# Another hand-written order for a fused retention and SoLU kernel: the same steps, rearranged over five engines

## The chip, the cores and the metric

The kernel runs on one core of a Trainium2 chip. A core has five engines that run their own instruction streams in order: PE (matrix multiplies and transposes), DVE (vector), ACT (scalar functions), POOL (GpSimd) and SP, which here only issues DMA transfers. They meet through semaphores. The metric is the device time of one execution in microseconds; the median of three runs before the change was 212.04 us (211.69 to 212.27).

## What is computed

Two parts follow each other. A retention layer works on q, k and v of 8 batches, 8 heads, 576 positions and 64 columns; its output, 4608 tokens of 512, goes through a feed-forward block with a SoLU activation and a layer norm.

```python
scores = scale * np.matmul(q, k.transpose(0, 1, 3, 2))
gamma = 1.0 - 2.0 ** (-5.0 - np.arange(H, dtype=np.float32))
Dmat = np.where(rel >= 0, gamma[:, None, None] ** rel[None, :, :], 0.0)
ret = scores * Dmat[None, :, :, :]
x = np.matmul(ret, v)
...
h = x @ w_in
sm = exp(h - max(h)) / (sum(exp(h - max(h))) + 1e-09)
solu = h * sm
ln = (solu - mean(solu)) / np.sqrt(var(solu) + 1e-06) * g_ln
out = ln @ w_out
```

The last six lines are shortened; `h` has 1024 columns, `out` has 512.

## The kernel before

The 4608 tokens are cut into 36 chunks of 128. For each pair of batches there are nine: four chunks of each batch in turn, and a ninth that holds the last 64 tokens of both. Each chunk passes through the same chain of steps, and each step is a small function with a two-letter name:

- `lq`, `lk`, `lv`: SP loads q, k and v of the chunk (256 KB each). `li` and `lo` load the four slices of w_in and of w_out (512 KB each).
- `cq`, `cv`: scale by a table of gamma powers and round to 16 bits; `ck`: round only. The engine is written behind the name: `a` ACT, `v` DVE, `g` POOL.
- `tq` (PE) transposes q and k into a PSUM bank, `eq` copies both halves out; `tr` and `er` do so for q alone where k is transposed by a DMA (`kd`, and `kq` for q).
- `sc` (PE, line 391) makes the scores in two PSUM banks, `mk` (DVE, line 404) masks them in two halves, `av` (PE, line 466) multiplies with v.
- `kv` (PE), `ad` (DVE), `dk` and `d3` (POOL) carry the running state of keys and values to the next chunk; `fs` (PE) adds its share to the output of `av`; `ex` copies the result out as xT.
- `m1` (PE, line 258) makes h, 128 by 1024, in one of two PSUM buffers; `mr` does the same in four parts, for the first two chunks, as the slices of w_in come in, each cast by `wi`.
- `mx` (DVE, line 522) takes the maximum, `xp` (ACT, line 528) the exponential, `so` (DVE, line 537) the product u, `sq` (ACT) the squares. The first five chunks are centred by `ce` (DVE); for the others, centred weights take its place.
- `tu` and `eu` transpose u through PE and copy it out; `du` does so by a DMA.
- `m2` (PE, line 258) multiplies with w_out, `st` (ACT) scales by the normalization and SP stores the chunk. The normalization is made by `ra` (a pair of small instructions, lines 576 and 582) and `rp` (POOL, line 591).
- `wo` scales w_out by g_ln, `mm` and `mc` make its mean over the rows, and the eight `ws` (line 831) subtract that mean: the centred weights w_c, which `m2` takes from chunk 5 on.
- The last chunk is worked in halves: `hm`, `hx`, `hp`, `ho`, `hc`, `ht`, `he`, `hq`, `h2`, `hw`.

The order is written out by hand in the string `ORDER`: 1021 tokens of the form step:chunk:engine, run from left to right under a manual schedule. Each engine gets its instructions in that order and executes them in that order; a step that waits holds up all that stand behind it on its engine. SP issues loads, stores and transposing DMAs in the same way, so a store that waits for its data holds up the loads behind it. Two more strings are consumed alongside: `BANKS` names one of four PSUM banks for each allocation in turn, and `SLOTS` names the buffer in a ring for each tile. A new tile in a bank or slot waits until the last reader of the old one is done.

Of the kernel before, what the change touches and what calls it, by code (L numbers as in the profile page):

```python
# [28 lines left out]
so:1 ce:1 mx:0 fs:2 tq:3 dk:2 ex:2:a d3:2 eq:3:a lk:8 sq:1 m1:2 cv:3:g ad:4 xp:0 mx:2 kv:3 av:4
fs:4 lq:7 ck:5:g ad:3 sc:3 cq:5:g so:0 ex:4:a mk:3 tq:5 tu:1 dk:3 xp:2 dk:4 lq:10 cv:5:g d3:3  # L30
eq:5:a lv:7 cq:6:g lq:11 m1:4 sc:5 d3:4 wu:3:1 wo:1:g cv:6:g wo:5:g wo:0:g av:3 wo:3:g eu:1:a
ce:0 wo:7:g so:2 mk:5 tu:0 mx:4 ck:6:a sq:0 eu:0:a fs:3 tq:6 ra:1:g av:5 fs:5 ra:0:g lq:8 ex:3:a
kv:5 lq:20 ad:5 eq:6:av rp:1 d3:5 m1:3 xp:4 cq:7:g kv:6 dk:5 rp:0 sc:6 ex:5:a ce:2 wo:4:a tu:2
lk:9 so:4 ad:6 m1:5 lq:9 mk:6 ce:4 sq:2 av:6 ra:2:g wo:2:a fs:6 wo:6:a mx:3 xp:3 lv:9 tu:4 lv:8
# [6 lines left out]
st:3 so:6 mk:9 fs:8 ck:12:a cv:12:g m2:5 ex:8:a av:9 sc:10 so:7 m1:8 sq:6 ex:9:v tu:7 cv:10:v  # L41
lv:20 mk:10 tu:6 cq:12:g st:5 m1:9 mx:8 ra:6:v sq:7 lv:14 lv:27 eu:6:a xp:8 eu:7:v lq:15 lk:14
kv:10 ad:10 av:10 kv:11 lv:13 lv:15 ck:13:g ex:10:a so:8 ra:7:g ad:11 mx:9 tq:11 rp:7 lv:21 m2:7
lq:16 lk:17 lk:18 lk:15 cq:17:g tu:8 eq:11:v sq:8 rp:6 eu:8:v m2:6 st:7 tq:12 sc:11 xp:9 eq:12:a
lk:20 ra:8:g so:9 m1:10 st:6 dk:9 sq:9 mk:11 cv:18:g d3:11 lq:23 av:11 mx:10 sc:12 fs:11 dk:11
ck:16:a xp:10 dk:10 mk:12 ex:11:a m2:8 rp:8 cq:13:g tu:9 av:12 st:8 lv:17 so:10 cq:14:g ra:9:g
# [46 lines left out]
0123102310102310321032013203112032120312031312310213002130213023013021032102313210213012301320132032  # L93
3012032031231023120311203132012310321032130210320130021302123012032103210320120123012302130213012301
30121320101320313012303123102310320
# [7 lines left out]
vf 012345601234560125436154164305216425  # L103
kf 012345012345012340152341503215401235
qf 012345601234560135260315246031564023
k16 012345021345023145021543210541403251
q16 012340123401204312431201204413410421
v16 012340132401324301340132410140312432
t 01231021302132013201320132012310
qkT 012302130213102310231203213213102310  # L110
s16 012312031203102310230123012031203
ret0 012302130213021302130213021302130123
ret1 012302130213021302130213021302130123
# [762 lines left out]
```

## Time and profile before

| | us |
|---|---|
| median of three runs | 212.04 |
| the profiled execution | 212.92 |
| its span, first to last instruction | 210.6 |
| PE busy | 191.4 |
| DVE busy | 180.7 |
| ACT busy | 167.1 |
| POOL busy | 167.8 |
| bytes moved by DMA | 47.97 MB |

A row of the page's groups gives line, engine, operation, the tile written and those read, shapes and count; behind the bar stand busy time, mean duration in nanoseconds, and idle time of the engine just before, with what ended it. In the chain of waits and in the timeline each row begins with start and length in microseconds; a bracket at the end of a timeline row gives the idle time before it and what ended it. One matmul step as `m1` is recorded as 16 instructions that overlap, so durations of PE are read from start to start.

### The profile page before, as it was taken

The page shows a single profiled execution, that of the slowest core. Times are in us where ns is not written, and L with a number is a line of the kernel's source. Part 1 is how long each engine was busy: PE and PEld are TensorE (multiplying, and loading weights), DVE is VectorE, ACT ScalarE, POOL GpSimd, SP SyncE. Part 2 cuts the span into 40 slices and gives each one's busy share as a digit, 9 for nine tenths or more (in the row PEclk, how much of TensorE's full clock was granted, in tenths as well). Part 3 has the DMA queues.
Part 4 walks back from the last instruction along what each step waited for, and adds up shares of the span by engine and source line. Part 5 has one row for each costly group of instructions (what it writes and reads, how often), then busy time and mean ns, then how long its engine had stood idle before and what let it go on. Part 6 is the DMA issues. An engine that isn't in the chain of part 4 may idle for free.

```text
span 210.6 us, 7529 instructions
## 1 busy us (share of the span) xinstructions
PE 191.4 (91%) x3091; PEld 122.7 (58%) x3091; DVE 180.7 (86%) x303; ACT 167.1 (79%) x293; POOL 167.8 (80%) x252
## 2 busy tenths in 40 slices
PE   0387889899889999999999999999999999999992
PEld 0353566665656667566666566675664665655571
DVE  0366999999999997998999899999999899899730
ACT  2266799789867788799888789999896999878961
POOL 3455999999999499899989999699939999851530
PEclk9999999999999999999999999999999999999998
DMA  6999999999999999999848999999899999993942
GB/s 156 306 300 248 257 284 347 244 241 228 210 291 336 232 238 234 282 241 253 243 110 242 191 207 267 224 266 162 179 237 178 207 219 240 162 265 85 239 157 100
DMA packets 111858, 47.97 MB, mean 228 GB/s; under 512 B 95560, under 2 KB 105808, under 8 KB 111824
## 3 DMA queue, kind: packets, MB, share of 16 engines
q1 hardware_dynamic: 111504, 47.33, 96.7%
q8 instruction: 24, 0.39, 0.8%
q10 hardware_dynamic: 320, 0.16, 0.3%
q14 instruction: 10, 0.08, 0.1%
HBM read 32.54 MB, written 9.44 MB: 199 GB/s over the span
## 4 chain that ended last, share of the span: by engine, by line
PE 69%; DVE 15%; SPq 6%; DMA 4%; ACT 2%; issue 1%; POOL 1%; ACTq 0%; DVEq 0%
PE o L258 26%; PE h L258 23%; PE tp L253 5%; PE sc L391 4%; DMA vf<-in_v_dram 4%; DVE nm L522 4%; DVE u L537 3%; PE x L466 3%; PE x L258 3%; SPq L270 3%; DVE ret L404 3%; PE lp L253 3%; DVE w_c L831 2%; PE kp L415 2%; SPq L274 1%; SPq L789 1%
## 5 line engine op out<-in xcount | busy, mean ns | idle before, releaser
L258 PE MATMUL h<-w_in,xT 128*64 128x512 f16 x560 | 68.6, 385 | 1.9 <-ACT w_in L245 0.9
L258 PE MATMUL o<-w_c,uT 128*64 128x512 f16 x480 | 56.7, 380 | 0.0
L404 DVE TENSOR_TENSOR ret<-sc,tris 128x512 f16<-128x512 f32 x72 | 46.0, 681 | 1.8 <-PE sc L391 1.3
L258 PEld LDWEIGHTS <-xT 128*64 128x64 f16 x576 | 31.4, 111 | 25.4 <-issue 3.0
L528 ACT ACTIVATE e<-h,nm 128x1024 f32<-128x1024 f32 x35 | 39.1, 1117 | 8.7 <-DVE nm L522 7.4
L258 PEld LDWEIGHTS <-uT 128*64 128x64 f16 x560 | 31.3, 110 | 22.6 <-issue 0.4
L537 DVE SCALAR_TENSOR_TENSOR u<-h,e 128x1024 f16<-128x1024 f32 x35 | 42.5, 1215 | 1.8 <-ACT e L528 1.7
L522 DVE TENSOR_REDUCE nm<-h 128x1 f32<-128x1024 f32 x35 | 42.6, 1216 | 1.0 <-PE h L258 0.9
L288 POOL TENSOR_TENSOR v<-vf,small 128x512 f16<-128x512 f32 x32 | 33.7, 1059 | 10.1 <-DMA vf<-in_v_dram 7.7
L565 ACT ACTIVATE sq<-u,su 128x1024 bf16<-128x1024 f16 x30 | 34.5, 1149 | 3.0 <-DVE u L537 2.9
L442 POOL TENSOR_TENSOR s<-t,small 128x512 f16<-128x512 f32 x32 | 33.1, 1043 | 1.7 <-DVE t L430 1.5
L299 POOL TENSOR_TENSOR q<-qf,small 128x512 f16<-128x512 f32 x30 | 32.0, 1071 | 0.3
L245 ACT COPY qkT<-tp 128x512 f16<-128x512 f16 x45 | 24.3, 591 | 9.4 <-PE tp L253 9.3
L625 ACT ACTIVATE o_sb<-o,rs 128x512 f32<-128x512 f32 x35 | 24.0, 687 | 5.6 <-POOL rs L591 2.4
L591 POOL TENSOR_TENSOR rs<-w,mhalf 128x1 f32<-128x1 f32 x36 | 20.2, 563 | 4.7 <-DVE su L685 3.2
L253 PE MATMUL tp<-ident,q 128*64 128x128 f16 x248 | 13.1, 229 | 9.5 <-DVE q L299 7.7
L253 PEld LDWEIGHTS <-q 128*64 128x64 f16 x280 | 11.2, 115 | 13.1 <-DVE q L299 8.2
L245 ACT CAST xT<-x 128x512 f16<-128x512 f32 x25 | 14.7, 587 | 4.1 <-PE x L258 2.5
L391 PE MATMUL sc<-qkT 64*128 64x128 f16 x288 | 14.6, 225 | 1.6 <-ACT qkT L245 1.0
L466 PE MATMUL x<-ret,v 128*64 128x128 f16 x288 | 14.6, 222 | 0.9 <-DVE ret L404 0.8
L582 POOL TENSOR_SCALAR w<-ss,w 128x1 f32<-128x1 f32 x24 | 6.4, 265 | 11.1 <-ACT sq L565 8.8
L454 POOL TENSOR_TENSOR s<-t,small 128x256 f32<-128x256 f32 x24 | 14.8, 620 | 0.2
(86 smaller groups left out, 273.3 us busy)
## 6 DMA issues: line engine op xcount, KB each, us to landing
vf<-in_v_dram SPq DMA_DIRECT2D x36, 256.0 KB, 5.2
kf<-in_k_dram SPq DMA_DIRECT2D x36, 256.0 KB, 5.1
qf<-in_q_dram SPq DMA_DIRECT2D x36, 256.0 KB, 5.1
out_dram<-o_sb SPq DMA_DIRECT2D x35, 256.0 KB, 3.9
w_in<-in_moe_w_in_dram SPq DMA_DIRECT2D x4, 512.0 KB, 5.9
w_out<-in_moe_w_out_dram SPq DMA_DIRECT2D x4, 512.0 KB, 6.5
uT<-u SPq DMA_TRANSPOSE x18, 3.9
out_dram<-o_sbh SPq DMA_DIRECT2D x2, 64.0 KB, 2.1
```

What stands on the lines that cost most here:

```text
L245: (engine.copy if engine is nc.scalar else engine.tensor_copy)(out=out, in_=in_)
L253: nc.tensor.transpose(out=out[w], in_=in_[:, w], identity=ident)
L258: nc.tensor.matmul(out=out[w], lhsT=lhsT[:, w], rhs=rhs, start=start, stop=stop, skip_group_check=True,)
L288: engine.tensor_tensor(out=dst, in0=T.pop((key, n)), in1=table.unsqueeze(2).to_broadcast([P, H, D]), op=ALU.mult,)
L299: ENG[e].tensor_tensor(out=dst.rearrange("p (a h) d -> p h a d", h=2), in0=T.pop(("qf", n)).rearrange("p (h a) d -> p h a d", h=2), in1=ta ...
L404: nc.vector.tensor_tensor(out=r, in0=s, in1=m, op=ALU.mult)
L442: nc.gpsimd.tensor_tensor(out=s16, in0=t.unsqueeze(2).to_broadcast([P, 4, 2, D]), in1=gd.unsqueeze(3).to_broadcast([P, 4, 2, D]), op=ALU.mult,
L522: nc.vector.tensor_reduce(out=nm, in_=T["h", n], axis=AX.X, op=ALU.max, negate=True)
L528: nc.scalar.activation(out=e, in_=T["h", n], func=ACT.Exp, bias=T.pop(("nm", n)), accum_out=s)
L537: nc.vector.scalar_tensor_tensor(out=u, in0=T.pop(("h", n)), scalar=-1.0, in1=T.pop(("e", n)), op0=ALU.mult, op1=ALU.mult, accum_out=su,)
L565: nc.scalar.activation(out=s, in_=T.pop(("v", n)), func=ACT.Square, scale=-float(DFF), bias=T.pop(("su", n)), accum_out=ss,)
L625: nc.scalar.activation(out=o_sb, in_=T.pop(("o", n)), func=ACT.Copy, scale=T.pop(("rs", n)))
```

## The change

Only `ORDER`, `BANKS` and `SLOTS` are new; no function is touched. Both orders have 1021 tokens and the same steps on the same chunks. What differs is where a step stands, and for 63 of them on which engine it runs. Counted by engine (`eq` has two halves, each with its engine):

| step | before: ACT, DVE, POOL | after: ACT, DVE, POOL |
|---|---|---|
| ck | 18, 1, 17 | 17, 4, 15 |
| cq | -, 5, 31 | -, 3, 33 |
| cv | -, 4, 32 | -, 2, 34 |
| eq (halves) | 45, 17, - | 45, 17, - |
| er | 3, 1, - | 4, 0, - |
| ex | 25, 11, - | 29, 7, - |
| eu | 10, 7, - | 9, 8, - |
| ra | -, 7, 29 | -, 14, 22 |

`wi` and `ws` keep their counts; ws:2 and ws:0 swap POOL and DVE. The ra moved to DVE are those of chunks 5, 7, 18, 20, 25, 29, 32 and 35; that of chunk 26 goes to POOL.

The order of the first loads, and the steps up to the place where the prediction looks:

```diff
-c1:0 lv:1 lk:1 lq:2 lq:1 ck:1:g cq:1:v lk:2 lq:0 cv:1:v li:3 lk:0 cq:2:g lv:0 lq:4 li:0 ck:2:g
-li:2 lk:4 cv:0:g tq:1 kv:1 ad:1 eq:1:a ck:0:a sc:1 wi:3:1:v dk:1 li:1 cq:0:v tq:2 mk:1 eq:2:a
...
-kv:0 eq:0:a mr:1:3 ad:0 dk:0 wi:0:0:a wi:2:1:a mk:2 sc:0 mk:0 c2:0 d3:0 mr:1:0 wi:1:1:v ck:4:a
-d3:1 mr:1:2 wi:1:0:a tq:4 av:0 mr:1:1 ex:0:v lk:6 lv:5 cv:4:g mr:0:0 cv:2:g mx:1 eq:4:a lq:6 lo:0
...
-ex:6:a cq:10:g eu:2:v cv:7:g ck:7:v so:3 mx:5 sq:4 ra:4:g rp:2 lk:10 dk:6 lv:12 rp:4 m2:1 mm:0
-tq:7 mc:0:v eq:7:a xp:5 ce:3 m1:6 ck:9:g eu:4:v ws:4:g sc:7 ck:8:a cq:9:g st:1 ws:2:g lk:13 sq:3
-m2:0 lv:10 ws:3:v mk:7 lk:11 lk:12 lv:11 st:0 so:5 ck:10:g lq:12 ws:1:v lv:18 cv:8:g av:7 ra:3:g
-kv:7 fs:7 ad:7 cq:8:v ex:7:a sq:5 m2:2 dk:7 tq:8 cv:9:v lq:17 st:2 mx:6 eq:8:a rp:3 tu:5 tu:3
-cq:11:g lq:14 lk:16 kv:9 ws:5:v ad:9 ws:7:v ck:11:g m1:7 ws:6:v sc:8 eu:5:a eu:3:a m2:4 mx:7 xp:6
-lq:13 mk:8 cv:11:g ws:0:v xp:7 tq:9 d3:9 st:4 tq:10 m2:3 eq:10:a ra:5:g rp:5 eq:9:v av:8 sc:9
...
-hm:35:1 ra:31:v rp:30 st:30 m2:31 so:34 rp:31 hx:35:0 hx:35:1 sq:34 hp:35:0 rp:32 hp:35:1 ho:35:0
-rp:33 du:34 ho:35:1 m2:33 st:31 ht:35:0 m2:32 st:33 ra:34:v hc:35 hq:35:0:v he:35:0:v ht:35:1
-rp:34 hq:35:1:a he:35:1:v m2:34 st:32 ra:35:g h2:35:1 rp:35 h2:35:0 st:34 hw:35:1:v hw:35:0:a
+c1:0 lk:1 lv:1 ck:1:v lq:0 lq:1 lk:2 lq:2 cv:1:g ck:2:a li:3 lv:0 lk:0 kv:1 li:0 li:2 cq:1:v lq:4
+lk:4 ad:1 wi:3:0:a tq:1 eq:1:v sc:1 gt:0 li:1 mk:1 cq:0:g wi:3:1:v lv:4 lv:2 d3:1 cq:2:g tq:2
...
+wi:0:1:g eq:0:av lk:6 kv:0 ad:0 wi:0:0:a wi:2:0:v wi:2:1:a wu:3:1 lq:6 sc:0 mr:1:0 lo:0 ck:4:a
+mk:0 mr:1:2 wi:1:0:a cq:4:g dk:0 lv:6 av:0 wi:1:1:v d3:0 tq:4 mr:1:1 ex:0:v lo:1 mr:0:3 lo:2
...
+m1:5 av:6 ce:4 rp:1 ad:6 wo:2:a wo:4:a wo:6:a mx:3 dk:6 cv:7:g eu:2:a lq:8 tu:4 xp:3 eu:4:v fs:6
+ra:2:g rp:0 m2:1 rp:2 ex:6:a ck:7:a mx:5 lv:9 mm:0 tq:7 lv:11 lq:9 xp:5 so:3 lk:9 lk:10 cq:9:g
+mc:0:v eq:7:a ck:9:g st:1 ck:8:a ck:10:g ce:3 ws:6:v lv:8 lk:16 m1:6 sc:7 lq:18 sq:4 lk:11 sq:3
+ws:0:g ws:1:v ra:3:g ws:2:v ws:4:g lq:17 lq:12 mk:7 m2:0 cq:8:v st:0 rp:3 kv:7 ad:7 ra:4:g lk:13
+lk:17 av:7 lv:10 lk:12 cv:8:g so:5 fs:7 rp:4 lv:12 m2:2 ex:7:a tu:3 ws:5:v lq:14 st:2 ws:3:v tq:8
+dk:7 eq:8:a lv:18 cq:11:g cv:9:v tu:5 eu:3:v kv:9 cv:11:g m1:7 cq:12:g ad:9 ws:7:v mx:6 sq:5 sc:8
+mx:7 eu:5:a m2:4 xp:6 mk:8 ra:5:v tq:10 eq:10:v lq:13 xp:7 lq:15 so:6 tq:9 eq:9:a m2:3 sc:9 st:4
...
+rp:31 m2:31 rp:30 ra:32:v ra:33:g st:30 so:34 du:34 hx:35:0 sq:34 st:31 hx:35:1 m2:33 hp:35:0
+hp:35:1 m2:32 ho:35:0 ho:35:1 rp:32 hc:35 ra:34:v rp:33 rp:34 st:33 ht:35:1 ht:35:0 he:35:1:v
+he:35:0:v m2:34 hq:35:0:v h2:35:1 st:32 hq:35:1:a h2:35:0 st:34 ra:35:v rp:35 hw:35:1:v hw:35:0:a
```

`BANKS` and `SLOTS` follow the new order, with other numbers throughout.

More of the change, by code (lines that the diff above doesn't have):

```diff
@@ L29 @@
[L29 to L34, printed above, removed]
@@ L41 @@
[L41 to L46, printed above, removed]
@@ new lines @@
+eq:4:a sc:4 cv:4:g cv:2:g mr:0:0 mx:1 xp:1 mr:0:2 lo:3 kv:2 mr:0:1 mk:4 lk:7 ad:2 so:1 ck:3:a
+cq:3:g av:2 fs:2 ex:2:a ce:1 mx:0 d3:2 lq:7 dk:2 tq:3 kv:4 cv:3:g ad:4 m1:2 kv:3 eq:3:a mx:2
+cq:5:g sq:1 ck:5:g d3:4 ad:3 av:4 dk:4 lq:10 xp:0 fs:4 sc:3 so:0 ex:4:a xp:2 cv:5:g tu:1 dk:3
+tq:5 d3:3 cq:6:g mk:3 wo:1:g eu:1:a m1:4 wo:0:g eq:5:a cv:6:g wo:3:g wo:5:g ck:6:a lq:11 wo:7:g
+ce:0 sq:0 ra:0:g sc:5 so:2 av:3 mk:5 ra:1:g fs:3 cq:7:g tu:0 ex:3:a eu:0:a tq:6 av:5 mx:4 cq:10:g
+kv:5 ce:2 eq:6:av lk:8 fs:5 m1:3 xp:4 ad:5 ex:5:a sc:6 dk:5 kv:6 d3:5 sq:2 lv:7 so:4 tu:2 mk:6
@@ new lines @@
+fs:11 st:6 sc:12 m2:8 sq:9 ra:9:g rp:9 ex:11:a xp:10 tu:9 cq:14:g mk:12 tq:13 so:10 st:8 lq:19
+av:12 fs:12 eq:13:a m1:11 eu:9:v ck:14:v kv:12 sc:13 lq:23 dk:11 d3:10 ad:12 mx:11 ex:12:a tq:14
+sq:10 d3:11 cq:17:g m2:9 eq:14:av tu:10 lv:17 mk:13 kv:13 cq:16:g m1:12 ad:13 lq:21 ra:10:g av:13
+xp:11 st:9 cv:14:g rp:10 cq:15:g eu:10:a ck:15:a fs:13 ck:17:a sc:14 so:11 sq:11 d3:12 m2:10
+ex:13:a dk:12 mx:12 mk:14 tq:15 cv:20:v xp:12 lv:16 tu:11 ra:11:g rp:11 lq:27 lk:21 so:12 eq:15:v
+kv:14 eu:11:a st:10 ad:14 m1:13 av:14 lv:23 mx:13 lk:26 fs:14 sc:15 cv:15:g m2:11 lv:19 mk:15
@@ new lines @@
+d3:13 dk:13 lk:22 d3:14 ck:18:a kv:15 sq:12 ad:15 cq:19:v ex:14:a tu:12 tq:16 dk:14 tq:18 st:11
+ck:19:a dk:15 av:15 cq:20:g cq:21:g xp:13 eq:16:v lk:27 fs:15 cv:16:g ex:15:a m1:14 eu:12:v tq:17
+sc:16 so:13 eq:18:a lq:24 m1:15 eq:17:a mx:14 mk:16 cv:18:g kv:16 ra:12:g ad:16 lq:22 tu:13 sc:17
+dk:16 xp:14 mx:15 eu:13:a mk:17 sq:13 ra:13:v m2:12 av:16 ck:21:v tq:19 fs:16 ck:20:g cv:17:g
+rp:12 so:14 lk:24 xp:15 cq:27:g lk:23 cv:21:g m2:13 ex:16:a kv:18 st:12 eq:19:av tq:21 rp:13
+m1:16 ad:18 cv:19:g av:17 sq:14 fs:17 eq:21:va tq:20 so:15 mx:16 tu:14 st:13 kv:19 ra:14:g
@@ new lines @@
+ex:17:a ad:19 dk:19 eq:20:av dk:18 rp:14 xp:16 sq:15 lv:25 eu:14:v tu:15 ra:15:g so:16 lq:29
+d3:18 du:16 lv:28 cq:23:g lq:26 eu:15:a lq:25 lv:30 m1:17 ck:24:a sc:18 lv:24 sq:16 cq:22:g mk:18
+lv:22 lq:28 m2:14 rp:15 ck:27:a av:18 lk:30 lk:28 mx:17 xp:17 m2:15 ex:18:v ra:16:g st:14 sc:19
+mk:19 rp:16 m1:18 ck:22:g st:15 av:19 so:17 ex:19:a sc:20 mk:20 m2:16 sq:17 mx:18 av:20 fs:20
+tu:17 kv:20 ck:23:a m1:19 eu:17:v ra:17:g ad:20 xp:18 st:16 ex:20:a so:18 tq:22 tq:27 cq:29:g
+mx:19 sc:21 eq:22:a lk:25 m1:20 du:18 cq:26:g mk:21 cv:25:g mx:20 tq:23 sc:22 mk:22 eq:27:a xp:19
@@ new lines @@
+eq:26:a sq:21 so:22 st:19 sc:25 m1:24 mx:23 mk:25 xp:23 ad:24 cq:28:g sq:22 ck:30:g du:22 so:23
+sc:26 mk:26 ck:31:a du:23 mx:24 cv:28:g av:25 ra:21:g rp:21 fs:25 ex:25:a m2:21 sc:27 dk:24 m1:25
+ck:29:a cq:30:g kd:30 av:26 mk:27 kv:27 fs:26 lk:33 st:21 tq:29 tr:28 ad:27 lk:32 sq:23 xp:24
+ex:26:a mx:25 ra:22:g er:28:a m2:20 cq:31:g so:24 rp:22 cq:34:g rp:20 lq:33 eq:29:a xp:25 du:24
+st:20 sc:28 kv:28 m1:26 mk:28 tr:30 d3:27 lv:32 dk:27 av:28 ra:23:v av:27 ad:28 rp:23 sq:24
+cv:29:g er:30:a d3:28 ex:27:a cv:30:g m2:23 so:25 cq:32:g ex:28:a sq:25 lq:35 ck:32:g kd:31
@@ L90 @@
+hp:35:1 m2:32 ho:35:0 ho:35:1 rp:32 hc:35 ra:34:v rp:33 rp:34 st:33 ht:35:1 ht:35:0 he:35:1:v
+he:35:0:v m2:34 hq:35:0:v h2:35:1 st:32 hq:35:1:a h2:35:0 st:34 ra:35:v rp:35 hw:35:1:v hw:35:0:a
 """
 BANKS = """
[L93 to L95 removed]
+0123012301230123012301230123102301231023103203120132010321021302312130312301231230123021303210230121
@@ L96 @@
+0320130231203120312301302123021320312031312032012302132013201320102302310320130231203123023102310203
+10310201320132310213020131203021321
 """
@@ L102 @@
 SLOTS = """
[L103 to L113, printed above, removed]
+kf 012345012345012340315432051450213054
+vf 012345601234560132450325360453524136
+k16 012345021345023154021543025102514301
+qf 012345601234560134205316245016345021
+v16 012340132401324103240342310231423014
+q16 012340213402103421343102413402403124
+t 01230123012302130213021302130231
+qkT 012302130213102310231203210210312031
 h 010101010101010101010101010101010101
+ret0 012302130213021302130213021302103210
+ret1 012302130213021302130213021302103210
+s32 0123120132013201320123012
 xT 012301230123012301230123012301230123
-s32 0123021302103210321023012
+s16 012312013201320132010231023013201
 e 01201201201201201201201201201201201
-u 01234012304123041230412301432014302
-uT 01234012304213042130421304213042104
+u 01234012340123401234012341023410231
+uT 01234012340123401234102341032410324
 o_sb 01230123012301230123012301230123012
```

65 lines of the change are left out of this document (23 added, 42 removed).

## The prediction

> **What bounds the kernel now.** I read the page first for the shares of the whole span, then three stretches of it side by side, then the chain of waits at the place where one bound hands over to the other.
>
> ```profile
> span 210.6 us, 7529 instructions
> PE 191.4 (91%) x3091; PEld 122.7 (58%) x3091; DVE 180.7 (86%) x303; ACT 167.1 (79%) x293; POOL 167.8 (80%) x252
> ```
>
> ```profile
> 7.66:21.24 13.58, 10.52 (x139) 6.78 (x141) 7.57 (x16) 7.92 (x15) 6.67 (x8) 1.00 1.03 282
> 21.24:60.73 39.49, 35.17 (x602) 24.05 (x599) 38.91 (x62) 32.76 (x58) 38.48 (x49) 1.00 1.09 262
> 60.73:206.48 145.75, 145.75 (x2354) 91.92 (x2351) 133.16 (x224) 124.63 (x220) 119.10 (x182) 1.00 0.97 218
> ```
>
> Columns after the stretch and its length: busy time of PE, weight loads, DVE, ACT, POOL; granted clock, DMA share, GB/s. Four regimes follow. Up to 21.24 us no engine is full and the DMA share is 1.03: loads set the pace. From 21.24 to 60.73 DVE is busy 38.91 of 39.49 us while PE has 39.49 - 35.17 = 4.32 us of holes: DVE sets it. From 60.73 to 206.48 PE is busy in every microsecond, and no wait of PE is listed after 60.8. Behind 206.48 lies a tail of 210.6 - 206.48 = 4.1 us. The clock is 1.00 throughout, so it is no term.
>
> The hand-over is in the chain (start, length, what):
>
> ```profile
> 51.20 0.34 DVE w_c L831
> 52.55 1.57 DVE v L288
> 55.25 1.17 DVE w_c L831
> 59.48 0.61 DVE ret L404
> 60.13 0.64 PE tp L253 x16
> ```
>
> PE waits for the first half of mk:8 (the masking of chunk 8's scores, line 404), which frees the PSUM bank that the next transposes, tq:10, need; its second half frees the bank of m2:3 at 60.73. From there on the rest of the program runs as fast as PE issues.
>
> The start of the DVE regime is fixed by the last slice of w_in:
>
> ```profile
> 11.97 1.09 SPq L789 DMA_DIRECT2D w_in<-in_moe_w_in_dram  x1
> 19.91 0.62 ACT L245 CAST w_in<-w_in 128x512 f16<-128x512 f32 x1 [0.95 <-DMA w_in<-in_moe_w_in_dram]
> 20.58 1.05 PE L258 MATMUL h<-w_in,xT 128*64 128x512 f16 x8 [0.93 <-ACT w_in L245]
> 21.24 1.23 DVE L522 TENSOR_REDUCE nm<-h 128x1 f32<-128x1024 f32 x1 [0.29 <-PE h L258]
> ```
>
> **The change, part by part.** The sum is made against the profiled execution: 210.6 us of span, 212.92 us as its time, so 2.3 us lie around the span. The median of the runs is 212.04, that is 0.88 below; I subtract that at the end.
>
> *Start.* li:1, the slice above, stays the fourteenth issue of SP; ahead of it and with it there are in both orders ten loads of 256 KB and four of 512 KB. Swapped are only v with k of chunk 1, q of chunk 2 with q of chunk 0, k with v of chunk 0, and q of chunk 4 goes behind two slices of w_in. The first work of chunk 1 gets earlier (cv:1 moves to POOL, kv:1 ahead of tq:1, eq:1 to DVE), but it then waits for the same slice: in mr:1:1, the last quarter of the first h, and hence in mx:1 at 21.24. Cost 0. If the cover were gone, what the early chunk gains or loses is at most the 13.58 - 10.52 = 3.06 us of PE holes in that stretch; I let the anchor move by 0.3 either way.
>
> *DVE regime.* From mx:1 to mk:8 DVE does 44 steps in both orders. They are the same but for two: eu:2 and ck:7 go to ACT, and ws:2 and eu:3 come from POOL and ACT. eu:2 and eu:3 are the same copy and cancel. What is left is one cast against one subtraction:
>
> ```profile
> L831 DVE TENSOR_TENSOR w_c<-w_out,warm 128x512 f16<-128x512 f16 x6 | 4.9, 833 | 0.0
> L245 DVE CAST k<-kf 128x512 f16<-128x512 f32 x1 | 0.6, 647 | 0.0
> L245 DVE COPY uT<-lp 128x1024 f16<-128x1024 f16 x7 | 4.8, 680 | 0.0
> ```
>
> +0.83 - 0.65 = +0.19 us. Bounds: a subtraction took 0.34 at 51.20 and 1.17 at 55.25, so -0.3 to +0.5; I take the mean of six, +0.19.
>
> Inside the stretch the order shifts. cv:9 now has five of the six subtractions ahead of it instead of two, and eu:2 and ck:7 no longer: 3 x 0.83 - 0.68 - 0.65 = +1.2 us. Behind cv:9 on PE stand kv:9, m1:7, sc:8, m2:4 and tq:10, all held up with it.
>
> ```profile
> 54.26 0.32 PE L415 MATMUL kp<-v,k 128*64 128x64 f16 x8
> 54.38 1.92 PE L258 MATMUL h<-w_in,xT 128*64 128x512 f16 x16
> 56.80 0.40 PE L391 MATMUL sc<-qkT 64*128 64x128 f16 x8 [0.50 <-DVE t L428]
> 57.13 1.92 PE L258 MATMUL o<-w_out,uT 128*64 128x512 f16 x16
> 60.13 0.41 PE L253 MATMUL tp<-ident,q 128*64 128x128 f16 x8 [0.64 <-DVE ret L404]
> ```
>
> PE shows waits of 0.50 and 0.64 us between kv:9 and tq:10, so 1.14 us are swallowed and about 0.1 could show. If mk:8 came much earlier, kv:9 would be the wait and cost the full 1.2. I count 0, bound +0.1.
>
> The row of cv:9 itself, 1.57 us at 52.55, is drawn anew: the four of its kind on DVE have a mean of 0.98.
>
> ```profile
> L288 DVE TENSOR_TENSOR v<-vf,small 128x512 f16<-128x512 f32 x4 | 3.9, 980 | 0.0
> ```
>
> It may fall by 0.6 or stay; it stands again between subtractions and beside a busy POOL (38.48 of 39.49), so I take half, -0.3.
>
> *On ACT and POOL.* ACT gets eu:2 and ck:7 ahead of xp:5, about 1.0 + 0.6 us. It has room there: xp:3 waits 1.74 us for mx:3, and mx:5 itself moves up on DVE, with eu:2 and ck:7 gone.
>
> ```profile
> 42.40 1.11 ACT L528 ACTIVATE e<-h,nm 128x1024 f32<-128x1024 f32 x1 [1.74 <-DVE nm L522]
> ```
>
> Cover gone, so:5 would be late, at most by those 1.6. POOL trades ws:2 for ws:0, equal work.
>
> *PE regime.* The same 3091 matmuls are issued. Their neighbours matter little, but for sc:
>
> ```profile
> 161.99 0.33 PE sc L391 x8
> 175.99 0.55 PE sc L391 x16
> ```
>
> Two of them in a row take 0.55 instead of 0.66, so each visit to sc costs about 0.1. Both orders make 34 visits, and the 145.75 us stay. The moved normalizations (ra) go from POOL to DVE, net seven pairs, and behind mk:8 all of them:
>
> ```profile
> L582 DVE TENSOR_SCALAR w<-ss,w 128x1 f32<-128x1 f32 x7 | 1.5, 214 | 0.4
> L576 DVE TENSOR_SCALAR w<-s 128x1 f32<-128x1 f32 x7 | 1.4, 204 | 0.0
> L245 DVE CAST xT<-x 128x512 f16<-128x512 f32 x11 | 7.5, 684 | 0.5 <-PE x L258 0.4
> L245 DVE COPY qkT<-tr 128x512 f16<-128x512 f16 x1 | 0.7, 693 | 0.1
> L299 DVE TENSOR_TENSOR q<-qf,small 128x512 f16<-128x512 f32 x5 | 3.5, 706 | 5.7 <-DMA qf<-in_q_dram 5.7
> ```
>
> 7 x 0.42 = +2.9 us on DVE; against that four ex leave (-2.7), two cq (-1.4), two cv (-2.0), one er (-0.7), and three ck (+1.9) and one eu (+0.7) come: -1.3 in sum over the kernel. DVE is busy 133.16 of 145.75 us there, so neither the +2.9 nor the -1.3 meets the end; a ra that stands in front of a wanted step delays it by 0.42. SP's queue issues the same transfers; with DMA share 0.97 a load that lands late would stall PE, but most loads now stand as early as before relative to the stores, or earlier; a few, as v of chunks 25 and 32, stand later. Cost 0; bounds 0 to +0.6, a wait as long as the longest of PE above: nothing can be gained where PE never waits.
>
> *Tail.* st:31 now stands ahead of hp:0 on ACT, and st:32 ahead of the second hq:
>
> ```profile
> 197.31 3.45 PE o L258 x32
> 198.54 0.69 ACT L667 ACTIVATE eh<-hh,nm 128x512 f32<-128x512 f32 x1 [0.21 <-DVE nm L660]
> 203.91 0.55 POOL L591 TENSOR_TENSOR rs<-w,mhalf 128x1 f32<-128x1 f32 x1
> 205.72 0.48 DVE L735 TENSOR_SCALAR o_sbh<-oh,rs 128x256 f32<-128x256 f32 x1 [2.25 <-PE oh L258]
> ```
>
> The two o passes from 197.31 are m2:31 and m2:33; m2:31 ends at about 199.04. st:31 must wait for it, so hp:0 starts at about 199.7 instead of 198.54. Queued behind it are hp:1, ho, ht and both he; ht now stands behind m2:32 on PE, one pass of 1.73 us later, which hides it. The last rs, ready at 203.91 + 0.55 = 204.46, comes some 1.1 us later, at about 205.6, just before the 205.72 at which it is read. I count +0.1, bounds 0 to +0.4.
>
> *Sum.* 0 + 0.19 + 0 - 0.3 + 0 + 0.1 = -0.0. From 212.92 that is 212.9 for a profiled execution, and less 0.88 a median of 212.0.
>
> **A rule that speaks against it.** The 0.34 and the 1.17 for one and the same subtraction are the row to explain. The Trainium skill, page "SBUF — State Buffer", section "Who interferes with whom", says that VectorE and GpSimd share one port pair as a lock held for a whole instruction, and that a VectorE instruction with two SBUF inputs, or a cast in a 2-port mode, is stopped entirely by a GpSimd instruction that reads SBUF. The spread from 0.34 to 1.17 agrees with that. By it the count of such steps matters: it is 13 before mk:8 in both orders, so the sum stands; three of them standing together is the second rival below.
>
> **The rivals.**
>
> 1. *Faster, at the hand-over.* Steps of DVE miss POOL's multiplications: cv:9 falls to 0.98 (-0.6) and two of the six subtractions take 0.34 instead of 0.83 (-1.0). mk:8 comes by 0.19 - 1.6 = -1.4; kv:9 by 1.2 - 1.6 = -0.4, and PE behind it sheds its 1.14 us of waits, so it keeps up. With the tail -1.3: 210.7. For it: mc:0 and the subtractions come some 0.6 us sooner. Against: POOL has only 1 us of idle time in the whole stretch. No more than PE's 4.32 us can be won.
>
> 2. *Slower, at one place.* ws:6, ws:1 and ws:2 stand together directly ahead of mk:7, POOL works beside them without a break, and each takes the 1.17 of the row at 55.25. Against the mean that is 3 x 0.34 = +1.0; mk:7, mk:8 and all PE work behind them are late by it, and cv:9 keeps its 1.57 (+0.3 on my sum): 213.3. It decides from the second of the three that is held. For it: the 38.48 us of POOL. Against: the same mix of lengths was drawn before.
>
> 3. *Slower, in the PE regime.* A wait opens anew between 60.73 and 206.48, through a buffer whose slot was drawn anew, a load, or a ra ahead of a copy; once or twice the 0.50 to 0.64 that PE's waits took, +0.5 to +1.2: 212.9. For it: no margin is visible in a stretch filled to 145.75 of 145.75. Against: DVE has more room right behind mk:8: up to mk:10, ws:0, ex:9 and cv:10 leave, and ra:5 and ck:11 come.
>
> 4. *It doesn't move the start.* The new first loads buy nothing, since li:1 decides. This is part of my forecast, not apart from it.
>
> **How the numbers follow.** About 0.3% (0.64 us) is what this kernel's runs, 211.69 to 212.27, can tell from no change. Forecast (no change, 212.0): 0.44. Rival 1: 0.29. Rival 2: 0.16. Rival 3: 0.11. Half of rival 3 and a little of 2 stay within the bound and are balanced by forecasts that miss it, so faster 0.30, same 0.43, slower 0.27. The forecast alone reaches 211.4 to 212.7. The range takes in rival 1's 210.7 and rival 2's 213.3: 210.7 to 213.3.
>
> **What would show it.** DVE's first mx starts at 21.2 (start). mk:8 ends between 60.2 and 61.0, and PE shows no wait behind it (hand-over, PE regime). kv:9 starts near 55.3. hp:0 starts near 199.7 with PE's last pass still about 145.7 us behind m2:3 (tail). The prediction is wrong if mk:8 ends before 59.9 or behind 61.4, if mx:1 moves by over 0.3, or if PE waits over 0.6 us behind m2:3.

## The result, and the profile after

The new order takes 211.53 us as the median of 15 runs (210.59 to 212.37). The order before, in the runs beside it, takes 212.92 us (211.69 to 214.31, 15 runs). The ratio is 0.993, with a 95% interval of 0.9907 to 0.9953: faster by 1.4 us, or between 1.0 and 2.0. The 212.04 us from which the prediction set out was the median of the first three of these runs; the other twelve lie higher. Ratios and intervals in this document leave out the few executions that are over 1.5% longer than the fastest of their kernel.

The profiled execution took 211.82 us. That is 1.7 us more than its span; in nearly all runs on record this difference is 1.7 to 1.9 us, but in the profiled execution of before it was 2.3. So the pair of profiles differs by 1.1 us in time and only by 0.5 us in span. The page's first lines, then three stretches cut at the places that answer to those of before (start to the first maximum, on to m2:3, on to the tail):

```profile
span 210.1 us, 7522 instructions
PE 190.7 (91%) x3091; PEld 121.3 (58%) x3091; DVE 178.1 (85%) x312; ACT 167.8 (80%) x296; POOL 166.3 (79%) x240
```

```profile
7.66:21.38 13.72, 10.19 (x134) 6.58 (x135) 8.86 (x19) 6.08 (x11) 7.63 (x11) 1.00 1.02 284
21.38:60.26 38.88, 34.38 (x600) 23.47 (x598) 37.84 (x62) 33.13 (x58) 37.95 (x49) 1.00 1.13 266
60.26:206.00 145.74, 145.72 (x2359) 90.81 (x2354) 130.53 (x229) 126.81 (x226) 116.75 (x169) 1.00 0.98 218
```

The regimes are those of before. The third is as long as it was, 145.74 against 145.75 us, and full of PE; the view of waits lists none on PE behind m2:3. The first is 0.14 longer in this pair of executions, the second 0.61 shorter. All that this pair shows lies ahead of m2:3.

The hand-over in the timeline of PE after (start, length, step; in brackets the idle time ahead of it):

```profile
53.46 0.64 PE L253 MATMUL lp<-ident,u 128*64 128x128 f16 x16
55.31 0.32 PE L415 MATMUL kp<-v,k 128*64 128x64 f16 x8 [1.22 <-POOL w L580]
55.44 1.92 PE L258 MATMUL h<-w_in,xT 128*64 128x512 f16 x16
57.29 0.40 PE L391 MATMUL sc<-qkT 64*128 64x128 f16 x8
57.62 1.92 PE L258 MATMUL o<-w_out,uT 128*64 128x512 f16 x16
59.37 0.39 PE L253 MATMUL tp<-ident,q 128*64 128x128 f16 x8
...
60.26 1.89 PE L258 MATMUL o<-w_out,uT 128*64 128x512 f16 x16
```

kv:9 (55.31) now stands still for 1.22 us. The row names a small POOL instruction, but what ends just ahead of it is cv:9 on DVE, at 55.17. The waits of 0.50 and 0.64 us between kv:9 and tq:10 are gone: cv:9 has taken their place, and m2:3 comes 0.47 us sooner all the same. From kv:9 on PE runs without a hole to m2:3, so m2:3 is now fixed by the end of cv:9, 5.09 us ahead of it, and no longer by mk:8, which ends 0.19 us ahead of it. DVE's steps of that stretch, from its timeline after:

```profile
47.24 1.93 DVE L831 TENSOR_TENSOR w_c<-w_out,warm 128x512 f16<-128x512 f16 x3
50.29 1.51 DVE L299 TENSOR_TENSOR q<-qf,small 128x512 f16<-128x512 f32 x1
53.20 1.37 DVE L831 TENSOR_TENSOR w_c<-w_out,warm 128x512 f16<-128x512 f16 x2
54.49 0.68 DVE L288 TENSOR_TENSOR v<-vf,small 128x512 f16<-128x512 f32 x1
58.80 1.27 DVE L404 TENSOR_TENSOR ret<-sc,tris 128x512 f16<-128x512 f32 x2
```

cv:9 (54.49) takes 0.68 us where it took 1.57 in the chain of before, cq:8 (50.29) takes 1.51, and mk:8 ends at 60.07. The tail, from the timeline of ACT after:

```profile
199.03 0.67 ACT L625 ACTIVATE o_sb<-o,rs 128x512 f32<-128x512 f32 x1
199.60 0.68 ACT L667 ACTIVATE eh<-hh,nm 128x512 f32<-128x512 f32 x1
```

st:31 stands ahead of hp:0, which starts at 199.60 instead of 198.54.

One number of the description is to be put right: 65 steps run on another engine in the new order, not 63.

### The profile page after: what moved, and what is told of

Same layout as the page of the kernel before. It is cut to its first block, busy times and chain, and to the rows that moved or that the text cites. A ratio compares the mean times of both kernels' runs of the same rounds, so it can differ in the third digit from the quotient of the medians.

```text
span 210.1 us, 7522 instructions
## 1 busy us (share of the span) xinstructions
PE 190.7 (91%) x3091; PEld 121.3 (58%) x3091; DVE 178.1 (85%) x312; ACT 167.8 (80%) x296; POOL 166.3 (79%) x240
## 4 chain that ended last, share of the span: by engine, by line
PE 69%; POOL 14%; SPq 6%; DMA 4%; issue 2%; ACT 1%; DVE 1%; POOLq 0%; ACTq 0%
PE o L258 25%; PE h L258 24%; PE tp L253 5%; PE sc L391 4%; DMA vf<-in_v_dram 4%; PE x L466 3%; SPq L789 3%; PE x L258 3%; POOL q L299 3%; PE lp L253 2%; POOL s L442 2%; POOL w_out L814 2%; POOL v L288 2%; SPq L274 2%; PE kp L415 2%
## 5 line engine op out<-in xcount | busy, mean ns | idle before, releaser
L404 DVE TENSOR_TENSOR ret<-sc,tris 128x512 f16<-128x512 f32 x72 | 46.0, 681 | 4.8 <-PE sc L391 4.7
L258 PEld LDWEIGHTS <-uT 128*64 128x64 f16 x560 | 30.1, 110 | 23.4
L288 POOL TENSOR_TENSOR v<-vf,small 128x512 f16<-128x512 f32 x34 | 35.7, 1055 | 5.5 <-DMA vf<-in_v_dram 5.2
L442 POOL TENSOR_TENSOR s<-t,small 128x512 f16<-128x512 f32 x32 | 33.7, 1056 | 6.8 <-DVE t L428 4.4
L299 POOL TENSOR_TENSOR q<-qf,small 128x512 f16<-128x512 f32 x32 | 33.2, 1043 | 2.1 <-DMA qf<-in_q_dram 1.9
L245 ACT CAST xT<-x 128x512 f16<-128x512 f32 x29 | 16.9, 587 | 4.3 <-PE x L258 2.3
L415 PE MATMUL kp<-v,k 128*64 128x64 f16 x256 | 9.6, 199 | 8.6 <-POOL v L288 7.4
L245 ACT CAST k<-kf 128x512 f16<-128x512 f32 x17 | 10.7, 635 | 7.5 <-DMA kf<-in_k_dram 7.5
L415 PEld LDWEIGHTS <-k 128*64 128x64 f16 x256 | 8.6, 114 | 12.3 <-DVE k L245 4.9
L391 PEld LDWEIGHTS <-qkT 64*128 64x128 f16 x288 | 8.5, 97 | 11.5 <-issue 6.2
```

The lines of the kernel that those rows point to most:

```text
L245: (engine.copy if engine is nc.scalar else engine.tensor_copy)(out=out, in_=in_)
L258: nc.tensor.matmul(out=out[w], lhsT=lhsT[:, w], rhs=rhs, start=start, stop=stop, skip_group_check=True,)
L288: engine.tensor_tensor(out=dst, in0=T.pop((key, n)), in1=table.unsqueeze(2).to_broadcast([P, H, D]), op=ALU.mult,)
L299: ENG[e].tensor_tensor(out=dst.rearrange("p (a h) d -> p h a d", h=2), in0=T.pop(("qf", n)).rearrange("p (h a) d -> p h a d", h=2), in1=ta ...
L391: nc.tensor.matmul(out=s[e][:, hp], lhsT=qkT[dd, 1, hp], rhs=qkT[dd, 0, hp], start=True, stop=True,)
L404: nc.vector.tensor_tensor(out=r, in0=s, in1=m, op=ALU.mult)
```

## The experiments

In orders put together from both, `BANKS` and `SLOTS` are written so that each tile follows the one that it followed in the order from which its stretch was taken; the program is a line shorter there, so L403 is the line shown as L404 above.

### Both orders again, and the two halves

Two theories. H: all of the gain lies ahead of m2:3. L: much of it lies behind, in executions whose transfers land late.

```
head_after    up to m2:3: new     behind it: old
head_before   up to m2:3: old     behind it: new
```

> The kernel before, profiled once more. Its runs spread from 211.7 to 214.3 us, its first profile was taken in a run of 212.92 us, and there PE had no wait behind m2:3. Theory H (the difference is made before the hand-over at m2:3): in an execution that is longer than 212.9, m2:3 starts later than 60.73 by the difference, and PE still has no wait behind it. Theory L (transfers that come late in the PE regime): m2:3 stays near 60.7 and PE shows waits behind it, for loads or for a transposing DMA, as long as the difference.

> The changed kernel beside the same runs of the kernel before as the two hybrids: ratio 0.993 by both theories, and PE without a wait behind m2:3 at about 60.3 us.

> The new order up to m2:3 (the last wait of PE in both profiles), and all that is left in the old order. Theory H: the whole gain, ratio 0.993, m2:3 near 60.3. Theory L: the profiled pair's 0.5 us at most, ratio 0.998, with waits of PE behind m2:3 in the long executions.

> The old order up to m2:3, and all that is left in the new order. Theory H: no gain, ratio 1.000. Theory L: the larger part of the gain, ratio 0.995 to 0.996.

Measured: the order before 212.29 us in one run, which is not the long execution that would have told H from L; the new one 211.45 (ratio 0.9944, 0.9912 to 0.9976), head_after 0.9981 (0.9952 to 1.001), head_before 1.003 (0.9992 to 1.0069). Neither half alone has the gain. H wanted all of it in head_after, which has a quarter to a third; L wanted some in head_before, which is rather slower than the order before. The profiled execution of head_before was its slowest, 218.03 us where the median is 213.45; its waits of PE behind the hand-over:

```profile
PE o L257 <- DMA uT<-u: 1.7, 1, 1.7
PE tp L252 <- DVE ret L403: 0.6, 1, 0.6
PE sc L390 <- DVE qkT L244: 0.4, 1, 0.4
```

The 0.4 stands in the profile of mid_before below too, at 212.28 us. It is nearly a wait of the size that the prediction named for its third rival, in orders that are spliced. The other two were seen in this one long execution alone, and nothing is concluded from them.

### Three parts, all eight ways

The head was cut once more at m1:2, the first whole h of a third chunk (25.47 us before). Theory D: the DVE stretch between m1:2 and m2:3 carries everything. S: the first loads carry half. J: transfers issued ahead across a cut matter.

```
              up to m1:2   to m2:3   behind
mid_after     old          new       old
start_before  old          new       new
mid_before    new          old       new
start_after   new          old       old
```

> The order of before up to m1:2, the new order from there to m2:3, the old one behind it. Theory D (the vector stretch carries the whole gain: m1:2 to m2:3 takes 34.3 us instead of 35.25, and the rest is draw): ratio 0.9955, stretch 34.3 to 34.7 in the profile. Theory S (the first loads carry half of it or more, in executions whose first loads land late): 0.998 to 1.000.

> The order of after, but the old order up to m1:2. Theory D: nothing is lost, 0.9935 to 0.995 as for after. Theory S: the gain of the first loads is lost, 0.997 to 0.998, and the runs spread as widely as those of before (2 us and more between the lowest and the highest quarter's ends).

> The order of after, but the old order between m1:2 and m2:3. Theory D: the whole gain is lost, 0.999 to 1.000, the stretch back at 35.2 us. Theory S: 0.997, half of the gain stays. Theory J (the transfers issued ahead across the two cuts matter, so that no single part gains what the whole does): above 1.000.

> The order of before, but the new order up to m1:2. Theory D: 1.000. Theory S: 0.997, with m1:2 at 25.4 us or earlier in the profile. Theory J: 1.000 to 1.003.

| start, middle, rest | ratio | 95% interval | m1:2 to m2:3 | m2:3 to m1:34 |
|---|---|---|---|---|
| old old old | 1 | | 35.26 | 130.57 |
| new old old (start_after) | 0.9964 | 0.9936 to 0.9991 | 35.26 | 130.56 |
| old new old (mid_after) | 0.9986 | 0.9953 to 1.0019 | 35.52 | 131.27 |
| new new old (head_after) | 0.9981 | 0.9952 to 1.001 | 34.68 | 130.93 |
| old old new (head_before) | 1.003 | 0.9992 to 1.0069 | 35.06 | 133.34 |
| new old new (mid_before) | 1.0008 | 0.9981 to 1.0035 | 35.24 | 131.22 |
| old new new (start_before) | 0.996 | 0.9924 to 0.9995 | 34.31 | 130.98 |
| new new new (again_after) | 0.9944 | 0.9912 to 0.9976 | 34.32 | 130.64 |

The last columns are starts on PE in one profile each, in us; that of old old old is before. again_after, head_after and head_before ran on one chip and the other four on a second, each beside the order before, so ratios are compared and not medians. With four ratios against four, the new middle is worth 0.9968 - 1.0001 = -0.0033, the new start 0.9974 - 0.9994 = -0.0020, the new rest 0.9985 - 0.9983 = +0.0002, each within about 0.002. So D and S both hold a part, and S's is about as large as its uncertainty. D's numbers for mid_after are missed, though: 0.9986 for 0.9955, and 35.52 us for the stretch; the next part says why.

The effect that J expects is there too, and more clearly than S's; whether transfers make it is another matter. The four ratios in which middle and rest come from one order have a mean of 0.9967, the four in which they are mixed 1.0001: a seam at m2:3 costs 0.0034, again within about 0.002, 0.7 us. In the profiles PE takes 130.56 to 130.98 us from m2:3 to m1:34 where the two come from one order and 130.93 to 131.27 where they are mixed (133.34 in the long execution of head_before), one profile each. So the middle and the rest can't be valued apart: the new middle is worth 0.9952 - 1.0019 = -0.0067 ahead of the new rest and 0.9984 - 0.9982 = +0.0002 ahead of the old one.

### Why the middle is shorter

The lengths in the middle are not drawn. From the start of mx:2 to the end of mk:8 DVE takes 33.04, 33.02, 33.04 and 33.02 us in four profiles with the old middle (before, again_before, start_after, mid_before), and 31.96, 31.96 and 31.95 in after, again_after and start_before, which have the new one. Every step in it repeats to 0.01 us or so; cv:9 takes 1.64 us in all four of the first and 0.68 in all three of the second. Two profiles with the new middle, head_after and mid_after, took longer; they come below. The timeline of before, DVE beside POOL:

```profile
51.23 0.77 POOL L245 CAST k<-kf 128x512 f16<-128x512 f32 x1
...
51.79 0.76 DVE L299 TENSOR_TENSOR q<-qf,small 128x512 f16<-128x512 f32 x1
51.97 1.60 POOL L831 TENSOR_TENSOR w_c<-w_out,warm 128x512 f16<-128x512 f16 x1
52.47 1.64 DVE L288 TENSOR_TENSOR v<-vf,small 128x512 f16<-128x512 f32 x1
53.52 1.49 POOL L299 TENSOR_TENSOR q<-qf,small 128x512 f16<-128x512 f32 x1
54.04 1.21 DVE L522 TENSOR_REDUCE nm<-h 128x1 f32<-128x1024 f32 x1
54.98 1.15 POOL L831 TENSOR_TENSOR w_c<-w_out,warm 128x512 f16<-128x512 f16 x1
55.17 1.24 DVE L831 TENSOR_TENSOR w_c<-w_out,warm 128x512 f16<-128x512 f16 x1
```

And of after:

```profile
50.22 1.04 POOL L299 TENSOR_TENSOR q<-qf,small 128x512 f16<-128x512 f32 x1
...
51.20 1.63 POOL L245 CAST k<-kf 128x512 f16<-128x512 f32 x2
...
52.80 1.16 POOL L831 TENSOR_TENSOR w_c<-w_out,warm 128x512 f16<-128x512 f16 x1
...
53.93 0.69 POOL L576 TENSOR_SCALAR w<-s 128x1 f32<-128x1 f32 x1
...
54.70 0.52 POOL L580 TENSOR_TENSOR w<-w,ss 128x1 f32<-128x1 f32 x1
```

Read them in pairs. Before, cv:9 begins at 52.47 while POOL's subtraction runs; that ends at 51.97 + 1.60 = 53.57, and cv:9 ends at 54.11, 0.54 later. POOL's next step, issued at 53.52, then takes 1.49 instead of the 1.04 of its like at 50.22 in after: it waited in its turn. The subtraction at 55.17 ends at 56.41, 0.28 behind POOL's at 56.13. In after the collision falls on cq:8: begun at 50.29, ended at 51.80, 0.54 behind POOL's q at 51.26. cv:9 (54.49) has only the two small instructions of a normalization beside it and goes through in 0.68, and it is the small one at 54.70 that stretches to 0.52. mx, which reads PSUM, takes 1.21 to 1.23 whatever POOL does. So in these rows a step of DVE with two operands in SBUF that begins while a POOL instruction of 512 columns runs ends about 0.55 us (f32 operand) or 0.28 us (both 16 bits) behind it, and the two then take turns. The Trainium skill, page "SBUF — State Buffer", section "Who interferes with whom", has that rule (two SBUF inputs, or a 2-port mode, against a GpSimd instruction that reads SBUF; whoever issues first holds the lock to its end); these rows agree with it.

From start to start, cv:9 gives -0.97, ce:3 -0.39, ws:3 and ws:5 together -0.45, the exchange of eu:2 and ck:7 for eu:3 and ws:2 -0.48; cq:8 gives back +0.75, so:3 +0.31 (0.24 of it a wait of DVE for the mean that mc:0 takes from PE), three small ones +0.2. Sum -1.03 of the -1.07 measured. PE then gives back 0.14, since tq:9 now stands between tq:10 and m2:3.

head_after took 32.32 us and mid_after 33.16 for the same new middle. cv:9 and cq:8 are as in after; the `ce` are longer, in mid_after three of them. From the timelines of mid_after:

```profile
39.96 1.04 POOL L813 TENSOR_TENSOR w_out<-w_out,g 128x512 f16<-128x512 f32 x1 [0.79 <-DMA w_out<-in_moe_w_out_dram]
...
46.38 1.04 POOL L441 TENSOR_TENSOR s<-t,small 128x512 f16<-128x512 f32 x1
46.48 1.23 DVE L552 TENSOR_SCALAR u<-u,nmu 128x1024 f16<-128x1024 f16 x1
```

A slice of w_out landed late, POOL waited 0.79 us for it (0.29 in head_after), and its later steps met DVE elsewhere: ce:3 (46.48), which reads one 16-bit tensor, ends 0.29 us behind POOL's step (47.71 against 47.42) and takes 1.23 us instead of the 0.59 of after. So the same reading holds, but the two orders fix the meetings only while the loads land in time: here late loads cost 0.4 and 1.2 us.

A test of that reading: so:5 reads PSUM, so it can stand beside POOL's q in place of cq:8.

```diff
-mk:7 m2:0 cq:8:v st:0 rp:3 kv:7 ad:7 ra:4:g lk:13 lk:17 av:7 lv:10 lk:12 cv:8:g so:5 fs:7
+mk:7 m2:0 so:5 kv:7 ad:7 cq:8:v st:0 rp:3 ra:4:g lk:13 lk:17 av:7 lv:10 lk:12 cv:8:g fs:7
```

> The order of after with so:5 and ad:7 ahead of cq:8 on DVE; nothing else is moved. Theory K (a DVE instruction that reads two operands from SBUF and meets a POOL instruction waits for its end, and the two then take turns): the 1.43 us of cq:8 shrink to about 0.8, but ws:5, ws:3 and cv:9 then each meet a POOL instruction, and mk:8 ends 0.4 to 1.0 us later than in after; m1:2 to m2:3 takes 34.7 to 35.3 us. Theory R (lengths are drawn at random about their mean): cq:8 falls to its mean of 0.9 or so, the rest keeps its mean, and m1:2 to m2:3 takes 33.7 to 34.3 us.

```profile
50.85 1.16 POOL L244 CAST k<-kf 128x512 f16<-128x512 f32 x2
...
51.42 1.13 DVE L298 TENSOR_TENSOR q<-qf,small 128x512 f16<-128x512 f32 x1
51.98 1.59 POOL L830 TENSOR_TENSOR w_c<-w_out,warm 128x512 f16<-128x512 f16 x1
52.48 1.71 DVE L830 TENSOR_TENSOR w_c<-w_out,warm 128x512 f16<-128x512 f16 x2
```

Measured in one run: 211.37 us, and 34.28 us from m1:2 to m2:3, as in after. That misses K's 34.7 to 35.3. R's range holds the sum, but not its parts: cq:8 saves 0.37 from start to start (1.43 to 1.06), and ws:5, which in its turn meets POOL's subtraction, gives back 0.35 (0.95 to 1.30). K has the turn-taking right and the count wrong: POOL, no longer held by cq:8, did its two casts in 1.16 instead of 1.63 us, so ws:3 and cv:9 met small instructions again. The sum alone does not decide against R; the rows do.

### What fixes the start

In all seven profiles with the new sequence of first loads and v of chunk 2 in its place, m1:2 starts 3.13 or 3.14 us behind cv:2, which POOL begins as soon as v of chunk 2 has landed. The timeline of again_after shows the way:

```profile
21.34 1.28 DVE L404 TENSOR_TENSOR ret<-sc,tris 128x512 f16<-128x512 f32 x2
22.39 1.04 POOL L288 TENSOR_TENSOR v<-vf,small 128x512 f16<-128x512 f32 x1 [1.24 <-DMA vf<-in_v_dram]
23.49 0.32 PE L415 MATMUL kp<-v,k 128*64 128x64 f16 x8 [1.49 <-POOL v L288]
23.91 0.42 DVE L430 TENSOR_TENSOR t<-kp,s 128x256 f32<-128x256 f32 x1 [1.29 <-PE kp L415]
24.25 1.21 DVE L537 SCALAR_TENSOR_TENSOR u<-h,e 128x1024 f16<-128x1024 f32 x1
25.53 0.84 PE L258 MATMUL h<-w_in,xT 128*64 128x512 f16 x6
```

The transfer of v for chunk 2 starts cv:2, then kv:2 (23.49), ad:2 (23.91) and so:1 (24.25), whose end frees one of the two h buffers for m1:2. DVE stands still for 1.29 us ahead of ad:2. With the old loads the last slice of w_in lands at 19.6 to 20.6 us, in head_before's long execution at 22.2, and DVE's queue behind it (mx:1, mk:4) is about as late: m1:2 starts 3.1 us behind cv:2 in before and mid_after, but 3.39, 3.50 and 4.53 in again_before, start_before and head_before. With the new loads that slice lands at 18.7 to 19.5, in after at 20.0, and drops out of the race.

That m1:2 comes sooner by this is not shown: it starts at 25.1 to 26.3 us in the four ordinary profiles with the old loads and at 24.8 to 25.9 in the seven with the new ones. The gain of the start is seen in the medians; that it comes this way, by executions in which the slice is late, is argued.

Two tests. v2_first is the new order with v of chunk 2 loaded one place sooner, and what follows from it:

```diff
-lv:4 lv:2 ... cv:4:g cv:2:g ... so:1 ck:3:a cq:3:g av:2 fs:2 ex:2:a ... tq:3 kv:4 cv:3:g ad:4 m1:2 kv:3 eq:3:a ... xp:0
+lv:2 lv:4 ... cv:2:g cv:4:g ... so:1 av:2 fs:2 ex:2:a ck:3:a cq:3:g ... kv:4 cv:3:g ad:4 m1:2 tq:3 kv:3 ... xp:0 eq:3:a
```

first_loads is the old order with nothing changed but the sequence of its first 16 loads in SP's queue:

```diff
-lv:1 lk:1 lq:2 lq:1 lk:2 lq:0 li:3 lk:0 lv:0 lq:4 li:0 li:2 lk:4 li:1 lv:4 lv:2
+lk:1 lv:1 lq:0 lq:1 lk:2 lq:2 li:3 lv:0 lk:0 li:0 li:2 lq:4 lk:4 li:1 lv:4 lv:2
```

> The order of after with v of chunk 2 loaded ahead of v of chunk 4, and what follows from it: cv:2 ahead of cv:4, ex:2 ahead of ck:3, tq:3 behind m1:2, eq:3 behind xp:0. Theory V (m1:2 starts 3.20 us after v of chunk 2 lands, by way of cv:2, kv:2, ad:2 and so:1, and DVE waits 1.3 us for it): v of chunk 2 lands near 20.1 us instead of 22.3, ad:2 follows mk:4 without the wait, m1:2 starts near 24.2, m2:3 near 58.7, and the ratio to before is 0.988 (0.985 to 0.992). Rival W (the last slice of w_in sets the start, as the prediction had it): v of chunk 2 has slack, nothing changes, m1:2 stays at 25.4 to 25.6, ratio 0.994. Rival X (the new phase of DVE and POOL costs up to 1 us behind it, as the old start did in front of the new stretch): 0.993 to 0.997 though m1:2 is early.

> The order of before, with the first 16 loads issued in the sequence of after; every other step stays where it was, on its engine. Theory L1 (the gain of the new start is in the loads: the last slice of w_in lands at 18.7 to 19.0 us instead of 19.6 to 20.5): it lands so here, mx:1 starts near 20.3, m1:2 at 25.1 to 25.5, and the ratio is 0.996 to 0.998 as in start_after. Rival (the gain is in the engines of the first casts, or is draw): ratio 0.999 to 1.002.

first_loads: 0.9975 (0.9952 to 0.9998). The slice of w_in landed at 19.1 us, mx:1 began at 20.80 and m1:2 at 25.68, since cv:2 began at 22.55 in that execution: each is a little behind what L1 wanted, while the ratio is in its range. A part of the gain seems to be in the sequence of the loads; the interval only just leaves out 1.

v2_first, from its timeline:

```profile
20.18 1.04 POOL L287 TENSOR_TENSOR v<-vf,small 128x512 f16<-128x512 f32 x1 [1.01 <-DMA vf<-in_v_dram]
22.63 0.42 DVE L429 TENSOR_TENSOR t<-kp,s 128x256 f32<-128x256 f32 x1
24.24 1.92 PE L257 MATMUL h<-w_in,xT 128*64 128x512 f16 x16 [0.57 <-DVE u L536]
...
39.60 1.33 DVE L552 TENSOR_SCALAR u<-u,nmu 128x1024 f16<-128x1024 f16 x1
39.61 1.04 POOL L813 TENSOR_TENSOR w_out<-w_out,g 128x512 f16<-128x512 f32 x1 [0.21 <-DMA w_out<-in_moe_w_out_dram]
```

Theory V is right step by step as far as m1:2: cv:2 at 20.18, ad:2 straight behind mk:4, m1:2 at 24.24, 1.3 us sooner than in again_after. But the ratio is 0.9954 (0.9934 to 0.9974), no better than the new order, and m2:3 starts at 59.48, 0.37 sooner than in again_after, where V wanted 58.7. X came true: from mx:2 to the end of mk:8 pass 32.61 us instead of 31.96. ce:4 (39.60) alone loses 0.86, since it now meets wo:7 on POOL and ends 0.28 behind it; others win a little.

So wo:7 was moved out of its way.

```diff
-wo:7:g ce:0 sq:0 ra:0:g sc:5 so:2 av:3 mk:5 ra:1:g
+ce:0 sq:0 ra:0:g sc:5 so:2 av:3 mk:5 ra:1:g wo:7:g
```

> v2_first with one step moved: wo:7, which POOL began at 39.61 us when its slice of w_out had landed, 0.01 us after DVE began ce:4, goes behind ra:0 and ra:1. Theory K (ce:4 waited for that POOL instruction: 1.43 us instead of 0.57): ce:4 takes 0.6 to 0.8, m1:2 stays at 24.2, from mx:2 to the end of mk:8 pass 31.7 to 32.1 us instead of 32.61, m2:3 starts at 58.6 to 59.0, and the ratio to before is 0.991 to 0.993. Rival (the time given back has another cause, as late transfers or the matmuls between): the stretch stays at 32.4 to 32.8 us, ratio 0.995.

```profile
31.60 3.22 PE L257 MATMUL h<-w_in,xT 128*64 128x512 f16 x16
...
35.18 1.29 DVE L403 TENSOR_TENSOR ret<-sc,tris 128x512 f16<-128x512 f32 x2 [1.11 <-PE sc L390]
41.55 2.23 POOL L298 TENSOR_TENSOR q<-qf,small 128x512 f16<-128x512 f32 x2
41.78 1.09 DVE L552 TENSOR_SCALAR u<-u,nmu 128x1024 f16<-128x1024 f16 x1
```

Measured: 0.9933 (0.9905 to 0.9961), 211.36 us, the lowest run 210.52. This is just beyond the far end of K's range and level with the new order; that it beats it is not shown. Its profile can't decide about ce:4: the loads were late (m1:2 at 25.16, not 24.2), and m1:4 took 3.22 us instead of 1.92, since the granted clock was down, 0.50 in each microsecond from 31 to 34 and 0.83 in the mean of this stretch:

```profile
30.00:40.00 10.00, 9.91 (x184) 6.74 (x185) 8.82 (x16) 9.23 (x16) 9.92 (x12) 0.83 1.03 313
```

DVE waited 1.11 us there, and ce:4, so shifted, met POOL's next multiplication (41.55). The stretch took 32.00 us with that wait in it.

## Why the prediction was near in its number and wrong in its reason

The number, 212.0, lies 0.5 us from the 211.53 measured, but that is luck: two things cancel. The sum said that nothing would be gained; 1.4 us were. And the 0.88 us that were taken off came from a median of three runs: over 15 runs the order before stands at 212.92, 0.88 higher. What happened is the case "faster by over 0.3%", which had 0.30; the mechanism is that of the first rival.

- *What bounds the kernel.* Right: four regimes, the second set by DVE, the third by PE without a hole.
- *Start, cost 0.* The anchor mx:1 moved by 0.14 us in the profiled pair, inside the bound; in again_after it stands at 20.20, a microsecond sooner. The reason failed: li:1 keeps its place in the queue, but with other loads around it it lands, in most profiles, about a microsecond sooner, and m1:2 then follows v of chunk 2. In the medians the new start is worth -0.0020, 0.4 us, and first_loads alone -0.0025.
- *DVE regime, +0.19 and -0.3.* This is the step that failed. The sum had -0.1; measured were -1.07 on DVE to the end of mk:8 and -0.93 to m2:3, by the profiles with and without the new middle. The prediction took mean rows, and half a redraw for cv:9. The rows are not drawn: which step of DVE meets which of POOL follows, to 0.01 us, from the two orders as long as the loads land in time. The rule was quoted, but only the number of such steps was counted, not whom they meet.
- *kv:9 held by cv:9, counted 0.* Right in kind: kv:9 waits for cv:9, and the waits behind it are gone. That the forecast of 55.3 was met at 55.31 is luck in part, since this execution began the stretch 0.46 us later (m1:2 at 25.93 against 25.47); in again_after kv:9 stands at 54.90. mk:8 was to end at 60.2 to 61.0 and ended at 60.07, in again_after at 59.65, which is under the 59.9 that the prediction gave as a sign of being wrong.
- *PE regime, 0.* Right in the profile: 145.74 against 145.75 us, no wait. That the new rest goes with the new middle, 0.0034 by the table, was not thought of. The ra moved to DVE do no harm.
- *Tail, +0.1.* hp:0 was forecast at 199.7 and started at 199.60; from the second h2 (205.41 before, 204.93 after) to the end of the span it is 5.2 us in both. The cover held, the cost is 0.
- *Rivals.* The first had the right mechanism, but kv:9 came 1.05 us later instead of 0.4 sooner and cq:8 gave 0.75 back. Of the second, only the first of the three subtractions met POOL: 1.93 us for all three. The third shows in spliced orders only, as the 0.4 us in mid_before.

By the profiles the middle gives 0.93 us. By the ratios it gives 0.0033 and the start 0.0020, 1.1 us together of the 1.4, if one takes the mean over old and new rests. The start's share rests on intervals of a size with itself and stays the less certain one; the way by which it comes is argued. Not told apart: how much of a seam's 0.7 us is the transfers and how much the engines' order.

## What to carry to other kernels

Where DVE and POOL are both full, don't cost a moved step by its mean: lay the two engines' timelines beside each other, mark the DVE steps that take two operands from SBUF, and those that, as `ce` here, go through a 16-bit tensor in SBUF, and walk both orders forward, since each such meeting costs up to the rest of POOL's instruction. A load that lands late shifts the meetings, so see how long the order lasts with one. Steps that read PSUM are the ones to put beside POOL's long ones. And a transfer that keeps its place in a queue does not keep its time: look at the landing, and at which buffer its last user frees.

## What the hardware showed that was not expected

- DVE and POOL repeat each other to 0.01 us over tens of microseconds: 31.96, 31.96 and 31.95 us for 37 steps in three executions whose start differed by 0.8 us. With a slice of w_out that POOL waited for, the same steps took 32.32 and 33.16 us.
- POOL's instructions of one column wait as well: the step of line 580 took 0.52 us beside cv:9 in after; free, it takes 0.19.
- A single core alone can lose its clock for a while: in the profile of v2_wo 0.50 was granted from 31 to 34 us, with 1.00 in the stretch of before, and one m1 took 3.22 us instead of 1.92. PE had stood still for 1.68 us up to 30.01; whether that is the reason is not shown.
